# Another written-out order for attention's steps, with the combine step cut in two

## The chip, the cores and the metric

The kernel runs on one core of a Trainium2 chip. The metric is the device time of one execution in microseconds (us), as a median of runs. Matmuls run on TensorE (PE in the profile, its weight loads PEld), elementwise work on VectorE (DVE), ScalarE (ACT) and GpSimd (POOL); SyncE (SP) issues nearly all DMAs. Matmul results go to PSUM, which has eight banks here, used by number.

## The reference, cut to what matters

Three stages follow each other: an attention without softmax whose weights decay with distance, a mixture of four experts weighted by given probabilities, and a bilinear layer with an output product. All in float32.

```python
# attention: 2 batches, 8 heads, 768 positions, head size 64; per block of the sequence
intra = (q_b @ k_b.T * Dmask) @ v_b            # Dmask[i, j] = lam ** (i - j) for i >= j
out_b = intra + (q_b * lam_pow) @ kv_state
kv_state = lam_block * kv_state + (k_b * rev_pow).T @ v_b
# experts: x (1536 x 512), e = 0..3
p = probs / (probs.sum(-1) + 1e-9)
out += p[:, e] * (relu(x @ w1[e]) @ w2[e])
# bilinear
y = ((x @ wa) * (x @ wb)) @ w3 @ w_out
```

## The kernel before, in words

The kernel takes the sequence in chunks of 128 positions (six to a head) and handles two heads at a time, which makes eight units: 0 to 3 for batch 0, 4 to 7 for batch 1. `SETS` (line 57) cuts a unit's six chunks into two or three sets, so a step such as `S.5.1` is unit 5, set 1. For a set of units there are these steps, each a small function:

| word | function, line | engine | what |
|---|---|---|---|
| `qk`, `kv` | load_qk 421, load_kv 427 | SP | loads into four buffers each; the next load waits for the oldest one freed |
| `S` | scores 436 | PE | keys by queries into two banks, one a head; shape 64*128 |
| `M` | masked 452 | DVE | scores times the decay mask |
| `K` | decay 462 | ACT | keys scaled in place by a row of the mask |
| `Q` | queries 468 | POOL | queries scaled in place by `lq` |
| `U` | states 477 | PE | scaled keys by values; shape 128*64 |
| `V`, `N` | spread 489, chain 500 | ACT, DVE | the states' recurrence, one chunk a step |
| `X` | combine 511 | PE | two groups into one bank: queries by states (shape 64*64, line 520), then masked scores by values (shape 128*64, line 526) |
| `A`, `B` | attended 532 | ACT, DVE | the result out of PSUM as a rounded part and a rest |

The first four units' results for 512 tokens are the input of the experts for that third of the tokens, and the first experts are woven into the same order: `L` loads a slice of expert weights (512 KB; three raw buffers), `H` (ACT) and `D` (DVE) split it, `I.k.p` and `Y.k.p` are the in- and out-products of slice k in two halves of six full matmuls (128*128, line 122), `Z` (DVE), `HH` (ACT), `HL` (DVE) lie between them. `PB` loads the routing weights as a row for all partitions; `Z` reads it.

The preparation: `lam` loads the eight decay factors through ACT's queue and makes two constants, `zero` on DVE and `first` on POOL (line 366). `mask.h` and `lq.p` are scans on DVE, and each mask reads `first`. `half` copies the factors per pair of heads. `probs` loads the router's probabilities through ACT's queue. `route.0` sums them on POOL (four operations, lines 401 to 404), `route.1` takes the reciprocal on DVE, `route.2` multiplies on POOL, `route.3` stores the result for `PB`. `idle.12.3` runs 12 warm-up matmuls on zeros.

What sets the order is a string, `ORDER` (line 33), which the loop at line 578 walks word by word. Every engine's queue, SP's and POOL's too, takes its instructions in the order in which the words issue them; there is no reordering by a scheduler. Float32 matmuls show as two records each in the trace, so a score step of four chunks and two heads has 16. A step's last digits are its PSUM banks. After the string the kernel goes on with experts' slices 8 to 31 and the later stages, from functions that the change does not touch.

Of the kernel before, what the change touches and what calls it, by code (L numbers as in the profile page):

```python
# [43 lines left out]
A.1.1 U.3.2.5 I.2.0 K.2.1 B.1.1 qk.4.0 V.3.2 V.4.0 N.3.2.0 L.5 N.4.0.1 L.6 U.2.1.6 S.3.2.5.7 V.2.1
N.2.1.0 X.2.1.6 M.3.2 Q.3.2 X.3.2.5 kv.6.0 A.2.1 K.5.0 B.2.1 S.5.0.7.6 kv.5.1 A.3.2 I.2.1 M.5.0 Q.5.0
PB.1 L.7 B.3.2 H.5 qk.4.1 S.4.0.7.6 Z.2 qk.6.0 U.5.0.5 Q.4.0 D.5 HH.2 Y.1.0 H.6 M.4.0 I.3.0 K.6.0 D.6
V.5.0 K.5.1 X.4.0.7 HL.2 X.5.0.6 kv.4.1 A.4.0 N.5.0.1 B.4.0 H.7 U.6.0.5 kv.6.1 U.5.1.7 Y.1.1 qk.6.1
A.5.0 D.7 L.8 qk.7.0 V.6.0 V.5.1 I.3.1 B.5.0 N.6.0.1 N.5.1.0 N.5.1.1 S.6.0.6.5 Z.3 Y.2.0 K.4.1 Q.6.0
M.6.0 HH.3 N.5.1.2 K.6.1 X.6.0.6 HL.3 S.4.1.5.7 kv.7.0 A.6.0 B.6.0 U.4.1.6 M.4.1 Q.4.1 Y.2.1 L.9 V.4.1
N.4.1.0 N.4.1.1 S.7.0.5.7 N.4.1.2 X.4.1.6 M.7.0 Q.7.0 K.7.0 U.7.0.5 kv.7.1 A.4.1 U.6.1.7 I.4.0 H.8  # L50
qk.7.1 V.7.0 B.4.1 V.6.1 qk.5.1 N.7.0.1 N.6.1.0 N.6.1.1 X.7.0.6 N.6.1.2 S.6.1.5.7 A.7.0 B.7.0 I.4.1
M.6.1 Q.6.1 K.7.1 X.6.1.6 Z.4 D.8 HH.4 HL.4 S.7.1.5.7 A.6.1 B.6.1 Y.3.0 L.10 Q.7.1 M.7.1 I.5.0 Y.3.1
I.5.1 S.5.1.6.5 Z.5 U.7.1.7 M.5.1 Q.5.1 I.6.0 HH.5 V.7.1 HL.5 H.9 Y.4.0 N.7.1.0 N.7.1.1 N.7.1.2 I.6.1
# [1387 lines left out]
```

## Time and profile before

| | |
|---|---|
| median of 3 runs | 795.87 us (795.38 to 796.43) |
| the profiled execution: time, span | 796.46 us, 794.7 us |
| PE busy | 786.7 us, 99% |
| DVE, ACT, POOL busy | 547.2, 333.5, 142.7 us |
| TensorE's granted clock | full in all 40 slices |
| DMA | 95.1 MB, 120 GB/s over the span |

All rows below come from the one profiled execution. In lists by time the columns are the start, the length, the engine (SPq and ACTq are the queues that issue DMAs), the line of the kernel, the operation, its output and inputs with their shapes, and how many were merged; in square brackets stands how long the engine was idle before and what ended that. In the chain, a line is a stretch on the path that ended last, and "issue" is time in which the engine waited for nothing that the profile shows. In windows, each engine's busy time is followed by its count, in the order PE, PEld, DVE, ACT, POOL; then come the granted clock as a share of full speed, the DMA share and GB/s.

### The profile page before, as it was taken

The page shows a single profiled execution, that of the slowest core. Times are in us where ns is not written, and L with a number is a line of the kernel's source. Part 1 is how long each engine was busy: PE and PEld are TensorE (multiplying, and loading weights), DVE is VectorE, ACT ScalarE, POOL GpSimd, SP SyncE. Part 2 cuts the span into 40 slices and gives each one's busy share as a digit, 9 for nine tenths or more (in the row PEclk, how much of TensorE's full clock was granted, in tenths as well). Part 3 has the DMA queues.
Part 4 walks back from the last instruction along what each step waited for, and adds up shares of the span by engine and source line. Part 5 has one row for each costly group of instructions (what it writes and reads, how often), then busy time and mean ns, then how long its engine had stood idle before and what let it go on. Part 6 is the DMA issues. An engine that isn't in the chain of part 4 may idle for free.

```text
span 794.7 us, 10384 instructions
## 1 busy us (share of the span) xinstructions
PE 786.7 (99%) x3968; PEld 644.1 (81%) x3968; DVE 547.2 (69%) x835; ACT 333.5 (42%) x570; POOL 142.7 (18%) x107
## 2 busy tenths in 40 slices
...
GB/s 268 250 312 155 106 172 173 211 175 209 212 198 98 115 200 186 81 92 80 95 90 107 92 106 94 106 93 93 93 107 146 86 21 54 2 0 1 6 47 54
DMA packets 42178, 95.10 MB, mean 120 GB/s; under 512 B 4752, under 2 KB 10128, under 8 KB 42128
## 3 DMA queue, kind: packets, MB, share of 16 engines
...
q8 instruction: 31, 0.51, 0.2%
...
q10 hardware_dynamic: 672, 0.03, 0.1%
...
## 4 chain that ended last, share of the span: by engine, by line
PE 96%; DMA 2%; ACT 1%; DVE 0%; issue 0%; SPq 0%; ACTq 0%
PE y L122 33%; PE h L777 19%; PE h L122 11%; PE o L122 8%; PE ab L122 5%; PE a L1237 5%; PE b L1237 5%; PE w L122 5%; PE a L526 2%; PE a L443 2%; DMA w_dram<-w_sum 1%; PE a L520 1%; DMA kv<-in_kv_dram 1%; PE a L483 1%; DVE ab L1085 0%
## 5 line engine op out<-in xcount | busy, mean ns | idle before, releaser
L122 PE MATMUL y<-zp,w 128*128 128x512 f32 x768 | 186.5, 389 | 0.0
L122 PEld LDWEIGHTS y<-zp,w 128*128 128x128 f32 x768 | 144.0, 188 | 30.6 <-ACT ya L856 0.2
L227 POOL TENSOR_TENSOR cv<-cv,raw 128x512 uint32<-128x512 uint32 x40 | 65.5, 1636 | 433.5 <-DVE cv L220 391.7
L797 ACT CAST zp<-z 128x512 fp32r<-128x512 f32 x64 | 39.8, 622 | 114.8 <-DVE z L792 114.7
L122 PE MATMUL o<-w_hi,z 128*128 128x512 f32 (+1 forms) x208 | 60.1, 373 | 0.2 <-DVE z L105 0.2
L801 DVE TENSOR_TENSOR zp<-z,zp 128x512 fp32r<-128x512 f32 x64 | 44.1, 689 | 17.9 <-ACT zp L797 16.5
L319 DVE SCALAR_TENSOR_TENSOR z<-h,pb 128x512 f32<-128x512 f32 x32 | 22.1, 691 | 47.2 <-PE h L122 46.9
L122 PE MATMUL h<-xl,wh 128*128 128x512 f32 x128 | 51.0, 398 | 0.0
L122 PE MATMUL y<-hl,wh 128*128 128x512 f32 x128 | 50.5, 395 | 0.0
L122 PE MATMUL h<-xh,wl 128*128 128x512 f32 x128 | 49.9, 390 | 0.0
L122 PE MATMUL y<-hh,wl 128*128 128x512 f32 x128 | 49.9, 390 | 0.0
L122 PE MATMUL y<-hh,wh 128*128 128x512 f32 x128 | 49.9, 390 | 0.0
L326 ACT CAST hh<-z 128x512 fp32r<-128x512 f32 x32 | 19.9, 621 | 63.8 <-DVE z L319 63.8
L102 ACT CAST wh<-raw 128x1024 fp32r<-128x1024 f32 (+1 forms) x33 | 33.9, 1027 | 25.8 <-PE y L122 22.3
L122 PEld LDWEIGHTS o<-w_hi,z 128*128 128x128 f32 x208 | 37.9, 188 | 7.4 <-DVE z L105 0.5
L105 DVE TENSOR_TENSOR wl<-raw,wh 128x1024 fp32r<-128x1024 f32 (+1 forms) x33 | 39.8, 1207 | 3.4 <-ACT wh L102 3.4
L790 DVE TENSOR_TENSOR z<-h,v 128x512 f32<-128x512 f32 x16 | 11.1, 691 | 42.4 <-ACT wf L102 28.3
L105 DVE TENSOR_TENSOR w<-w,w 128x512 fp32r<-128x512 f32 x32 | 35.6, 1112 | 4.9 <-ACT w L102 4.9
L122 PE MATMUL o<-w_lo,z 128*128 128x512 f32 (+1 forms) x104 | 38.2, 373 | 0.0
L122 PE MATMUL h<-xh,wh 128*128 128x512 f32 x128 | 34.8, 390 | 0.0
L792 DVE SCALAR_TENSOR_TENSOR z<-z,pb 128x512 f32<-128x512 f32 x48 | 33.2, 692 | 1.6
L201 ACT ACTIVATE cv<-raw 128x512 f32<-128x512 f32 x40 | 26.8, 670 | 9.2 <-DMA raw<-in_w3t_dram 5.7
(227 smaller groups left out, 1655.4 us busy)
## 6 DMA issues: line engine op xcount, KB each, us to landing
...
```

The source lines that it names most:

```text
L102: act.copy(out=hi, in_=src)
L105: eng.tensor_tensor(out=lo, in0=src, in1=hi.bitcast(F32), op=ALU.subtract)
L122: lambda i=i, a=a, b=b: pe.matmul(ps, a, b, start=(first and i == 0), stop=(last and i == n - 1))
L201: act.activation(out=singles[i], in_=raws["f", i][:, :, 1].bitcast(F32), func=ACTF.Abs)
L227: pool.tensor_tensor(out=b, in0=b, in1=raws.pop(("f", i))[:, :, 0], op=ALU.add)
L319: dve.scalar_tensor_tensor(out=z, in0=h_ps.pop(k)[0], scalar=0.0, in1=pb_t[k // KF, 0], op0=ALU.max, op1=ALU.mult)
L326: act.copy(out=hh, in_=h_t[k][0])
L777: pe.matmul(chain_ps[to], w, x, start=begins and j == 0, stop=j == len(seq) - 1, skip_group_check=True,)
L792: dve.scalar_tensor_tensor(out=z, in0=src, scalar=0.0, in1=pb_t[2 * n // KF, PAIR[m]], op0=ALU.max, op1=ALU.mult)
L797: act.copy(out=t[:, 0], in_=z)
L801: dve.tensor_tensor(out=t[:, 1], in0=z_of.pop((m, f)), in1=t[:, 0].bitcast(F32), op=ALU.subtract)
L1237: pe.matmul(t, w, x, start=i == 0 and n in (1, 2, 5), stop=i == len(seq) - 1, skip_group_check=True,)
```

## The change

`combine` is cut in two: `XI` (function `inter`) holds the queries-by-states matmuls and takes the bank, `XP` the masked-scores-by-values matmuls that add to the same bank. So other steps can stand between the two halves. `ORDER` is written anew: the same steps, with every `X` as an `XI` and an `XP`, in another order and with other bank numbers. Steps whose matmuls have one shape stand next to each other more often (`U` beside `XP`, `S` beside `S`, `I` and `Y` together), unit 0's scores come first on PE, and `probs` and `route.0` stand ahead of `lam`. The diff, with the middle of both orders cut:

```diff
@@ -31,27 +31,29 @@
 ORDER = """
-kv.0.0 lam idle.12.3 qk.0.0 kv.1.0 qk.1.0 qk.2.0 qk.3.0 probs half mask.0 kv.2.0 mask.1 L.0.0 mask.2
-lq.0 kv.3.0 K.0.0 mask.3 mask.4 lq.1 U.0.0.5 mask.5 S.0.0.6.7 V.0.0 mask.6 lq.2 mask.7 route.0 lq.3
-K.1.0 M.0.0 U.1.0.4 Q.0.0 N.0.0.1 S.1.0.0.1 V.1.0 route.1 N.0.0.2 route.2 N.1.0.1 X.0.0.6 Q.1.0 M.1.0
-N.1.0.2 S.2.0.7.2 N.0.0.3 kv.3.1 A.0.0 N.1.0.3 qk.3.1 B.0.0 K.2.0 S.3.0.5.4 Q.2.0 M.2.0 X.1.0.6 H.0.0
-Q.3.0 K.3.0 M.3.0 U.2.0.7 qk.0.1 A.1.0 U.3.0.0 D.0.0 L.0.1 V.2.0 V.3.0 K.3.1 B.1.0 X.3.0.5 kv.0.1
-N.2.0.1 route.3 S.3.1.6.4 A.3.0 N.3.0.1 N.2.0.2 L.1 U.3.1.1 Q.3.1 B.3.0 X.2.0.2 V.3.1 M.3.1 N.3.1.0
-N.2.0.3 X.3.1.5 A.2.0 H.0.1 B.2.0 S.0.1.6.7 PB.0 A.3.1 D.0.1 I.0.0 Q.0.1 K.0.1 L.2 B.3.1 qk.2.1 M.0.1
...
+kv.0.0 probs route.0 lam mask.1 qk.0.0 kv.1.0 mask.0 idle.12.3 half qk.1.0 qk.3.0 K.0.0 lq.2 qk.2.0
+S.0.0.6.0 mask.3 mask.2 K.1.0 lq.0 lq.1 Q.0.0 M.0.0 mask.4 U.0.0.5 U.1.0.7 V.1.0 mask.7 N.1.0.1
+S.1.0.1.6 route.1 N.1.0.2 V.0.0 N.0.0.1 kv.2.0 N.1.0.3 Q.1.0 N.0.0.2 M.1.0 XI.0.0.3 XP.0.0 kv.3.0 mask.6
+lq.3 L.0.0 mask.5 K.2.0 qk.3.1 L.0.1 S.3.0.2.1 S.2.0.4.7 XI.1.0.6 kv.3.1 K.3.0 N.0.0.3 route.2 M.2.0
+Q.2.0 A.0.0 M.3.0 U.3.0.4 XP.1.0 U.2.0.1 V.3.0 S.3.1.5.7 N.3.0.1 K.3.1 Q.3.0 XI.3.0.0 V.2.0 U.3.1.4
+V.3.1 L.1 M.3.1 A.1.0 Q.3.1 N.2.0.1 kv.0.1 H.0.1 XP.3.0 N.2.0.2 XI.2.0.2 B.1.0 A.3.0 N.3.1.0 N.3.1.1
+N.2.0.3 qk.2.1 XI.3.1.7 K.0.1 U.0.1.5 route.3 B.0.0 V.0.1 qk.0.1 XP.3.1 A.3.1 XP.2.0 H.0.0 B.3.0 B.3.1
+kv.2.1 A.2.0 kv.1.1 kv.3.2 S.0.1.6.7 D.0.0 M.0.1 H.1 Q.0.1 B.2.0 D.0.1 L.2 N.0.1.0 K.3.2 I.0.0 PB.0
+qk.1.1 I.0.1 Z.0 K.1.1 XI.0.1.3 HH.0 D.1 H.2 HL.0 S.2.1.1.0 M.2.1 S.1.1.7.6 K.2.1 U.1.1.5 XP.0.1 qk.5.0
+qk.3.2 I.1.0 A.0.1 I.1.1 kv.4.0 L.3 V.1.1 H.3 N.1.1.0 Q.1.1 M.1.1 L.4 B.0.1 XI.1.1.3 XP.1.1 kv.5.0 D.2
+U.3.2.7 U.2.1.6 PB.1 A.1.1 Z.1 S.3.2.2.5 L.5 Y.0.0 Q.2.1 HH.1 K.5.0 V.2.1 I.2.0 V.3.2 qk.4.0 K.4.0
+N.3.2.0 N.2.1.0 Q.3.2 M.3.2 HL.1 I.2.1 XI.3.2.2 H.5 B.1.1 H.4 D.3 D.5 XI.2.1.6 qk.6.1 U.4.0.3 XP.2.1
+V.4.0 XP.3.2 A.2.1 B.2.1 U.5.0.5 L.6 N.4.0.1 Z.2 kv.5.1 A.3.2 V.5.0 S.4.0.7.6 S.5.0.4.3 B.3.2 K.5.1
+Q.5.0 M.5.0 Y.0.1 kv.6.0 Y.1.0 M.4.0 Q.4.0 L.7 D.4 N.5.0.1 qk.7.0 XI.4.0.4 K.6.0 XI.5.0.6 U.5.1.7 XP.5.0
+U.6.0.5 qk.6.0 XP.4.0 H.6 D.6 A.4.0 V.6.0 V.5.1 kv.4.1 Y.1.1 A.5.0 B.4.0 HH.2 kv.6.1 qk.4.1 B.5.0 K.6.1
+I.3.0 L.8 N.5.1.0 H.8 HL.2 N.6.0.1 N.5.1.1 I.3.1 Y.2.0 N.5.1.2 Z.3 L.9 S.6.0.6.4 Q.6.0 K.4.1 M.6.0
+S.4.1.5.7 XI.6.0.6 qk.7.1 Q.4.1 XP.6.0 U.4.1.4 A.6.0 kv.7.0 V.4.1 M.4.1 N.4.1.0 N.4.1.1 N.4.1.2 HH.3
+S.7.0.7.5 B.6.0 M.7.0 XI.4.1.6 XP.4.1 K.7.0 U.6.1.4 Q.7.0 HL.3 A.4.1 U.7.0.7 V.7.0 V.6.1 N.6.1.0 N.7.0.1
...
+D.7 Y.3.1 HL.4 Z.5 D.8 HH.5 HL.5 D.9 I.6.0 I.6.1 Y.4.0 V.7.1 L.10 Z.6 HH.6 N.7.1.0 Q.5.1 Q.7.1 I.7.0
+Y.4.1 Y.5.0 I.7.1 Y.5.1 N.7.1.1 N.7.1.2 M.5.1 XI.7.1.6 XI.5.1.7 Z.7 HH.7 XP.7.1 A.7.1 B.7.1 HL.6 XP.5.1
+A.5.1 HL.7 B.5.1
 """
...
@@ -508,9 +510,8 @@
             op1=ALU.add,
         )
 
-    def combine(u, s, to):
+    def inter(u, s, to):
         c0, _, n, _ = chunks(u, s)
-        kvt, pt = kv_t.pop((u, s)), p_t.pop((u, s))
         qd = qk_t.pop((u, s))[:, 0].rearrange("p (c i) -> p c i", c=n)
         ps = bank(to, "a")[:, : n * P].rearrange("p (c i) -> p c i", c=n)
         c1 = 0 if c0 else 1
@@ -521,13 +522,18 @@
                     ps[r, c, :], entering(u, s, c)[r], qd[r, c, :],
                     start=c == c1, stop=False, skip_group_check=True,
                 )
+        x_ps[u, s] = ps
+
+    def combine(u, s):
+        _, _, n, _ = chunks(u, s)
+        kvt, pt = kv_t.pop((u, s)), p_t.pop((u, s))
+        ps = x_ps[u, s]
         for c in range(n):
             for j in range(2):
                 pe.matmul(
                     ps[j * D : (j + 1) * D, c, :], kvt[:, 1, c, j, :], pt[:, j, c, :],
                     start=False, stop=True, skip_group_check=True,
                 )
-        x_ps[u, s] = ps
 
     def attended(u, s, low):
         b, hp = divmod(u, HP)
@@ -561,7 +567,8 @@
         "U": states,
         "V": spread,
         "N": chain,
-        "X": combine,
+        "XI": inter,
+        "XP": combine,
         "A": lambda u, s: attended(u, s, False),
         "B": lambda u, s: attended(u, s, True),
         "L": lambda j, *half: load_half(*half) if half else load("j", j),
```

## Rows read from the trace of the kernel before

**Rows 1.** The page: TensorE's busy time, and the chain that ended last.
```profile
PE 786.7 (99%) x3968; PEld 644.1 (81%) x3968; DVE 547.2 (69%) x835; ACT 333.5 (42%) x570; POOL 142.7 (18%) x107
...
PE 96%; DMA 2%; ACT 1%; DVE 0%; issue 0%; SPq 0%; ACTq 0%
```

**Rows 2.** Windows by stage: stretch, its length, busy time of each engine.
```profile
0.00:94.00 94.00, 91.91 (x897) 72.32 (x898) 52.99 (x114) 35.65 (x80) 16.13 (x27) 1.00 0.68 227
94.00:200.00 106.00, 104.86 (x462) 86.48 (x462) 83.96 (x127) 59.63 (x92) 24.72 (x19) 1.00 0.51 182
200.00:400.00 200.00, 198.58 (x870) 162.80 (x871) 149.34 (x224) 91.51 (x149) 22.10 (x13) 1.00 0.43 138
400.00:600.00 200.00, 200.00 (x879) 163.84 (x878) 151.32 (x234) 79.97 (x135) 18.64 (x9) 1.00 0.28 93
```

**Rows 3.** The chain in order of time: start us, us, what.
```profile
12.90 1.54 PE a L443 x24
14.44 0.83 PE a L520 x12
15.27 1.02 PE a L526 x16
...
16.99 0.36 issue
...
18.38 0.65 PE a L443 x8
...
23.05 1.59 PE h L122 x6
...
35.93 0.59 PE a L526 x8
36.52 0.35 PE a L483 x12
...
57.71 0.50 PE a L483 x12
...
75.78 1.36 PE h L122 x6
```

**Rows 4.** Instructions of POOL in order of time, the start.
```profile
1.06 0.29 POOL L366 TENSOR_SCALAR_AFFINE_SELECT first<-zero 128x128 f32<-128x128 f32 x1 [0.63 <-DVE zero L364]
5.69 0.40 POOL L401 TENSOR_TENSOR dsum<-dp 128x12 f32<-128x12 f32 x1 [4.34 <-DMA dp<-in_probs_dram]
...
6.80 0.26 POOL L404 TENSOR_SCALAR dsum<-dsum 128x12 f32<-128x12 f32 x1
```

**Rows 5.** Instructions of DVE in order of time, the start.
```profile
3.71 0.34 DVE L388 COPY lamq<-lamb 64x4 f32<-64x4 f32 x2 [2.73 <-DMA lamb<-in_lam_dram]
4.08 1.05 DVE L381 TENSOR_TENSOR_SCAN mask<-lamb,first 128x128 f32<-128x128 f32 x3
...
8.30 1.29 DVE L459 TENSOR_TENSOR p<-a,mask 128x512 f32<-128x512 f32 x2 [0.32 <-PE a L443]
9.51 0.27 DVE L502 SCALAR_TENSOR_TENSOR st<-st,lq,a 128x64 f32<-128x64 f32 x1
```

**Rows 6.** Instructions and DMA issues of ACT in order of time, the start.
```profile
0.71 0.40 ACTq L363 DMA_DIRECT2D lamb<-in_lam_dram  x1
...
1.21 0.39 ACTq L397 DMA_DIRECT2D dp<-in_probs_dram  x1
...
8.34 0.91 ACT L466 ACTIVATE kv<-kv,mask 128x256 f32<-128x256 f32 x2 [0.91 <-DMA kv<-in_kv_dram]
```

**Rows 7.** Instructions of PE in order of time, the start.
```profile
8.90 1.08 PE L483 MATMUL a<-kv 128*64 128x64 f32 x16 [0.63 <-ACT kv L466]
9.91 1.16 PE L443 MATMUL a<-qk 64*128 64x128 f32 x16
11.00 0.87 PE L520 MATMUL a<-qk,st 64*64 64x128 f32 x12
```

**Rows 8.** The DMA issues of SP in order of time, 48 to 66 us.
```profile
56.70 0.54 SPq L430 DMA_DIRECT2D kv<-in_kv_dram  x1
...
62.58 0.55 SPq L430 DMA_DIRECT2D kv<-in_kv_dram  x1
```

**Rows 9.** The tile kv: from issue to landing over all its loads.
```profile
DMA to landing us min/median/max: 3.0/5.8/7.9
```

**Rows 10.** Instructions of ACT in order of time, 50 to 70 us.
```profile
60.76 0.69 ACT L466 ACTIVATE kv<-kv,mask 128x128 f32<-128x128 f32 x2 [3.71 <-DMA kv<-in_kv_dram]
...
66.69 0.80 ACT L466 ACTIVATE kv<-kv,mask 128x192 f32<-128x192 f32 x2 [0.65 <-DMA kv<-in_kv_dram]
```

**Rows 11.** Windows with the DMA rate, in GB/s, last.
```profile
8.50:12.50 4.00, 3.53 (x56) 3.03 (x58) 3.27 (x10) 0.96 (x3) 2.18 (x3) 1.00 1.06 404
30.00:33.50 3.50, 3.50 (x22) 2.59 (x24) 2.74 (x5) 2.25 (x7) 0.87 (x1) 1.00 1.06 387
38.00:44.00 6.00, 6.00 (x62) 4.10 (x63) 1.82 (x6) 1.33 (x4) 1.19 (x2) 1.00 0.93 271
44.00:50.00 6.00, 6.00 (x64) 4.52 (x66) 4.49 (x7) 4.38 (x9) 0.46 (x1) 1.00 1.01 347
...
61.50:62.50 1.00, 1.00 (x24) 1.00 (x25) 0.00 (x0) 0.00 (x0) 0.00 (x0) 1.00 0.00 0
```

More of the change, by code (lines that the diff above doesn't have):

```diff
@@ L39 @@
-N.2.0.1 route.3 S.3.1.6.4 A.3.0 N.3.0.1 N.2.0.2 L.1 U.3.1.1 Q.3.1 B.3.0 X.2.0.2 V.3.1 M.3.1 N.3.1.0
-N.2.0.3 X.3.1.5 A.2.0 H.0.1 B.2.0 S.0.1.6.7 PB.0 A.3.1 D.0.1 I.0.0 Q.0.1 K.0.1 L.2 B.3.1 qk.2.1 M.0.1
-H.1 L.3 U.0.1.5 I.0.1 N.3.1.1 kv.4.0 V.0.1 N.0.1.0 D.1 kv.1.1 qk.1.1 X.0.1.6 Z.0 L.4 qk.3.2 HH.0 I.1.0
-kv.3.2 A.0.1 HL.0 H.2 kv.2.1 B.0.1 S.2.1.7.5 D.2 I.1.1 Q.2.1 qk.5.0 H.3 M.2.1 Y.0.0 K.4.0 D.3 K.1.1
-S.1.1.6.7 Z.1 U.1.1.5 Q.1.1 Y.0.1 V.1.1 M.1.1 HH.1 H.4 N.1.1.0 HL.1 X.1.1.6 K.3.2 D.4 U.4.0.7 kv.5.0
@@ L44 @@
[L44 to L53, printed above, removed]
@@ L54 @@
-D.9 Y.4.1 Z.6 HH.6 I.7.0 HL.6 Y.5.0 I.7.1 Y.5.1 Z.7 HH.7 X.5.1.6 HL.7 X.7.1.5 A.5.1 B.5.1 A.7.1 B.7.1
+kv.0.0 probs route.0 lam mask.1 qk.0.0 kv.1.0 mask.0 idle.12.3 half qk.1.0 qk.3.0 K.0.0 lq.2 qk.2.0
+S.0.0.6.0 mask.3 mask.2 K.1.0 lq.0 lq.1 Q.0.0 M.0.0 mask.4 U.0.0.5 U.1.0.7 V.1.0 mask.7 N.1.0.1
+S.1.0.1.6 route.1 N.1.0.2 V.0.0 N.0.0.1 kv.2.0 N.1.0.3 Q.1.0 N.0.0.2 M.1.0 XI.0.0.3 XP.0.0 kv.3.0 mask.6
+lq.3 L.0.0 mask.5 K.2.0 qk.3.1 L.0.1 S.3.0.2.1 S.2.0.4.7 XI.1.0.6 kv.3.1 K.3.0 N.0.0.3 route.2 M.2.0
@@ new lines @@
+U.6.0.5 qk.6.0 XP.4.0 H.6 D.6 A.4.0 V.6.0 V.5.1 kv.4.1 Y.1.1 A.5.0 B.4.0 HH.2 kv.6.1 qk.4.1 B.5.0 K.6.1
+I.3.0 L.8 N.5.1.0 H.8 HL.2 N.6.0.1 N.5.1.1 I.3.1 Y.2.0 N.5.1.2 Z.3 L.9 S.6.0.6.4 Q.6.0 K.4.1 M.6.0
+S.4.1.5.7 XI.6.0.6 qk.7.1 Q.4.1 XP.6.0 U.4.1.4 A.6.0 kv.7.0 V.4.1 M.4.1 N.4.1.0 N.4.1.1 N.4.1.2 HH.3
+S.7.0.7.5 B.6.0 M.7.0 XI.4.1.6 XP.4.1 K.7.0 U.6.1.4 Q.7.0 HL.3 A.4.1 U.7.0.7 V.7.0 V.6.1 N.6.1.0 N.7.0.1
+Y.2.1 N.6.1.1 N.6.1.2 S.6.1.5.7 M.6.1 H.9 Q.6.1 Y.3.0 H.7 I.4.0 B.4.1 XI.6.1.6 XI.7.0.7 qk.5.1 XP.7.0
```

1 line of the change is left out of this document (added).

## Prediction

> **What bounds the kernel now.** I read the page first. TensorE is busy for 99% of the span, and the chain that ended last is 96% PE [rows 1]; beside TensorE no engine passes 69%. So the time is PE's work plus the few moments in which PE waits. The windows by stage come next [rows 2]: the attention order that is changed fills the first 94 us (the first group of the next stage starts at 93.9), and PE is idle there for about 2.1 us: 1.04 before its first matmul, 0.63 for a decay on ACT, 0.36 at 17.0 us. From 94 to 600 it idles 2.6 us in 506. That later part keeps its instructions and their order and runs at PE's pace, so a microsecond won or lost before 94 us arrives at the end whole. I take nothing from behind it.
>
> Then I read the chain in order of time, where one line is a run of matmuls of one shape and its length is start to next start [rows 3]. There the price of a shape shows. Scores (64*128): 24 records take 1.54, 8 take 0.65, so 55.6 ns each and 0.205 per run. The inter products (64*64): 0.83 for 12, of which I take 0.055 each and 0.145 per run (the 0.02 to 0.03 left is the edge of the merging). The intra products and states share 128*64: 1.02 for 16 and 0.59 for 8 give 54 ns and 0.15 per run; a states group of 12 costs 0.50 after another shape but 0.35 right after intra products, which is the 0.15 saved. Expert groups (128*128) of 6 take 1.59 between other shapes and 1.36 among their own kind, 0.225 per run.
>
> **The gain.** I split both orders into runs of one shape. Before there are 75: 17 inter, 26 states-or-intra, 16 scores, 16 full (warm-up counted). After there are 49: 12, 14, 13, 10. The instructions are the same ones (XI and XP are the two halves of X). So the price falls by 5 x 0.145 + 12 x 0.15 + 3 x 0.205 + 6 x 0.225 = 0.73 + 1.80 + 0.62 + 1.35 = 4.5 us. This is PE time on the path, nothing covers it, and I take it as certain to about 0.5.
>
> **What is late next: the start.** In the new order `route.0` stands ahead of `lam`, so on POOL the four small operations on the router's sums stand ahead of `first`, and every mask scan on DVE reads `first`. Before, `first` ran at 1.06; the sums could start at 5.69 only, since their 24 KB landed then, 4.4 us after the issue at 1.21, and took 1.37 to 7.06 [rows 4, 6]. After, the load is issued at 0.71 and lands near 5.1, the sums end at 6.5, `first` at 6.8, and the masks begin 2.8 us later than the 4.08 of before [rows 5]. From here with durations of before: mask.1 and mask.0 end at 7.6 (0.33 apart, 0.40 the last); K.0.0 takes 0.91 on ACT [rows 6], to 8.5; `half`, lq.2, mask.3 and mask.2 end at 8.9, K.1.0 then at 9.85; U.1.0 follows (16 records, 0.46) to 10.3, S.1.0 (1.09) to 11.4. PE has nothing else queued ahead of these: S.0.0 fills only 1.1 us. The inter products of unit 0 then need the third state, N.0.0.2. On DVE ahead of it: lq.0 and lq.1 (0.64), M.0.0 (1.21 apart from the next), mask.4 and mask.7 (0.65), the reciprocal and five chain steps of 0.2, the last 0.27 long; it ends at 12.55. XI.0.0 ends at 12.8 and XP.0.0 (1.02) at 13.85. Before, PE had the same five steps behind it at 12.9 less 0.07 [rows 3, 7], that is 12.83. One run is saved in this stretch (0.15, counted above), so the waits here are 1.15 us more than before's. If the 24 KB land at 4.6 it is 0.65; if `first` were not held at all, 0. The lam values, issued second now, land by about 5 (2.9 after their issue before [rows 4 to 6]) and are hidden behind `first`. The swap of qk.3.0 and qk.2.0 and the later L.0.0 cost nothing here: their users run after 13.8, the loads are issued by 6.
>
> **What is late next: loads.** SP issues loads in order, and each waits for its buffer. The trace shows how long one takes when little is ahead of it [rows 8 to 10]; its rows carry lines, so I name loads by counting them in the order: kv.7.1 (512 KB) is issued at 62.58 and ACT, waiting for it, starts at 66.69, so 4.1; kv.7.0 (256 KB) 56.70 to 60.76, so 4.06. At 370 GB/s (387 and 404 in two full stretches, 271 to 347 in others [rows 11]) the bytes are 1.4 and 0.7, and a fixed 2.7 to 3.35 is left. The shortest landing of all kv loads is 3.0, so a fixed 2.3 is the low end. I take 2.7, from kv.7.1, since nothing moved in the microsecond before it [rows 11], and 0.2 from the freeing matmul to the issue. Now PE's work between the event that frees the buffer and the use, with the prices above, against the load's path:
> (a) qk.1.1 for S.1.1: behind the end of XP.2.0 go kv.3.2, L.2, PB.0 and itself, 1.31 MB. Path 0.2 + 2.7 + 3.5 = 6.4. PE has S.0.1 0.65, I.0.0 and I.0.1 2.95, XI.0.1 0.59, S.2.1 0.65 and 0.24 of small waits = 5.1. Wait 1.4.
> (b) kv.5.1 for U.5.1: from XI.3.2's end, qk.6.1, L.6 and itself, 1.57 MB: 0.2 + 2.7 + 4.25 + decay 0.85 = 8.0. PE: XI.2.1 0.44, U.4.0 to U.5.0 1.48, two scores 1.09, two Y groups 2.95, two inter 0.59 = 6.55. Wait 1.4.
> (c) U.4.1: its decay K.4.1 now stands on ACT behind H.8, which waits for L.8. From XP.5.0's end kv.4.1, kv.6.1, qk.4.1, L.8, 2.1 MB: 0.2 + 2.7 + 5.7 + H.8 0.95 + decay 0.85 = 10.4, less 0.67 of PE work before XP.4.0 ends = 9.7; PE from there to U.4.1 has 5.67 + 1.54 + 0.37 + 0.59 = 8.2. Wait 1.5.
> (d) U.7.0 behind qk.7.1 and kv.7.0: 5.8 against 4.0 plus the 1.5 of (c): wait 0.35.
> (e) U.0.1: kv.0.1 is freed by XP.1.0; 0.2 + 2.7 + 0.7 + decay 0.64 = 4.25 against 3.5 of PE work. Wait 0.7.
> Sum 5.35. I.1.0 also hangs on PB.0: D.1 stands on DVE behind Z.0, which needs the router row. That path (7.5 from XP.2.0) just fits behind (a)'s wait, so it costs nothing more, but up to 0.8 if (a) vanishes. Small waits for banks (a product group that needs a bank DVE or ACT has not emptied yet) I put at 0.45. Before's 0.36 at 17.0 us goes. Bounds of the load waits: 0 and 8.
>
> **Sum.** -4.5 + 1.15 + 5.35 + 0.45 - 0.36 = +2.1 us on the profiled 796.46 (span 794.7 and 1.76 around it), 798.6. That run lies 0.6 above the median 795.87 of the three, so the forecast in the median's terms is 798.0.
>
> **A rule weighed.** The trace's loads leave 2.7 us beside their bytes at 370 GB/s [rows 8 to 11]. The Trainium skill, page DMA: Bandwidth & Descriptors, section Anatomy of one DMA, fits a load (on GpSimd's path) as about 2.0 us fixed plus its bytes at 436 GB/s. By that the five waits would be 1.05 together, by estimate, and the sum -2.2. The rows here come from SP's queue with its own backlog, and they decide for me.
>
> **Rivals.** (1) Loads in time: if buffers come free about 1.4 us earlier relative to the use, or the fixed part is nearer 1.5, none of (a) to (e) waits: -4.5 + 1.15 + 0.45 - 0.36 = -3.3, 792.6. For it: the fastest landing is 3.0 [rows 9]. Against: every load on which ACT is seen waiting took over 4. (2) A draw: fixed 2.3 and 404 GB/s shorten the five waits to 0.67 + 0.69 + 0.66 + 0.56 + 0.26 = 2.84, sum -0.4, 795.5. It decides below a fixed 2.4. (3) Heavier: fixed 3.35, as kv.7.0 shows, adds 0.65 to (a), (b), (e) and to (c) with (d): +2.6, so +4.7, 800.6; for it also the 271 GB/s of 38 to 44 us. (4) The change doesn't do what it says, because the 0.15 to 0.225 belong to each step's own start and not to the change of shape: then nothing is saved, +6.6, 802.5. The states group that costs 0.35 after intra products and 0.50 elsewhere speaks against it.
>
> **How the numbers follow.** Forecast 0.44 (its own range 796.8 to 799.3, half a microsecond on each of a few waits), rival 1 0.20, rival 2 0.20, rival 3 0.13, rival 4 0.03. What a measurement of this kernel can tell from no change is about 0.2%, 1.6 us. Slower by more than that, above 797.5: two thirds or more of the forecast's cases, with rivals 3 and 4 and a few of rival 2, 0.53. Faster, below 794.3: most of rival 1 and a part of 2, 0.22. Within: 0.25. The range leaves out the far ends of rivals 1 and 3: 793.0 to 800.4.
>
> **What would show it.** Right: the first scan at 6.5 to 7 us; XP.0.0 ending near 13.8; PE waiting at S.1.1, U.5.1, U.4.1 and U.7.0 for loads or for the decays behind them, 3.5 us or more in all; the next stage starting near 96; runs of 24 scores at 1.54 and so on. Wrong: PE's idle time before the next stage below 4 us, or that stage starting before 93; or a run of states after intra products at no less than 0.50 for 12.

## The result, and the profile after

The changed kernel takes 806.98 us as a median of four runs (802.08 to 809.04), beside 795.95 before: a ratio of 1.013, 95% interval 1.0084 to 1.0176. I had forecast 798.0 in 793.0 to 800.4. The profiled execution took 807.36 (span 805.6), 10.9 more than the one of before. One run of the version h1_warm_both below took 1317.6 us at a mean granted clock of 0.557 and is left out of every comparison.

The page first [rows 1]: TensorE's busy time, its granted clock in 40 slices, and the chain's shares by engine.

```profile
PE 789.4 (98%) x3968; PEld 647.9 (80%) x3968; DVE 545.6 (68%) x835; ACT 333.1 (41%) x570; POOL 143.0 (18%) x107
...
PEclk9899999999999999999999999999999999999999
...
PE 87%; DMA 7%; DVE 3%; ACT 1%; issue 1%; SPq 1%; ACTq 0%; DVEq 0%
```

PE does the same work and is busy 2.7 us longer; DMA's share of the chain is 7% in place of 2%; and a digit of the clock that was 9 before is 8. The windows by stage [rows 2] say where:

```profile
0.00:94.00 94.00, 84.96 (x810) 68.44 (x811) 50.68 (x111) 34.06 (x77) 16.34 (x27) 0.95 0.65 214
94.00:200.00 106.00, 106.00 (x516) 87.81 (x515) 76.42 (x117) 57.99 (x89) 23.14 (x17) 1.00 0.49 172
200.00:400.00 200.00, 196.86 (x864) 161.24 (x863) 148.82 (x222) 90.71 (x148) 21.50 (x14) 1.00 0.45 145
```

In the first 94 us PE is idle for 9.0 us in place of 2.1. The chain in order of time [rows 3] shows that the next stage starts at 103.14 and not at 93.92, so 9.2 of the 10.9 us arise ahead of it:

```profile
1.43 6.67 DMA qk<-in_qk_dram
...
8.15 1.92 PE a L445 x16
10.07 1.90 PE a L485 x32
...
24.58 0.54 SPq L432
...
25.16 0.60 SPq L165
...
25.86 0.38 SPq L305
...
26.28 5.98 DMA qk<-in_qk_dram
...
32.39 1.23 PE a L445 x8
...
34.88 4.92 PE h L124 x12
...
55.85 0.44 PE a L533 x8
56.28 0.23 PE a L485 x8
...
82.57 0.50 PE a L485 x12
...
99.34 1.90 PE a L521 x32
101.24 1.90 PE a L533 x32
103.14 2.04 PE h L124 x8
```

Read the lengths. Sixteen score records took 1.09 before; here they take 1.92 at 8 us. Twelve expert records (one group pair) take 2.95 between other shapes; at 34.88 they take 4.92. Late in the order (82.57 on) every run has the price that I had put on it. Windows with TensorE alone (stretch, length, busy time, granted clock, DMA share, GB/s) name the reason:

```profile
8.00:12.00 4.00, 3.85 (x50) 0.57 1.06 402
...
9.00:11.00 2.00, 2.00 (x29) 0.50 1.06 398
...
12.00:32.00 20.00, 17.31 (x232) 1.00 0.84 262
32.00:40.00 8.00, 7.61 (x37) 0.57 0.50 180
40.00:103.00 63.00, 60.40 (x560) 1.00 0.57 189
```

A clock of 0.57 is one of 1.00 (2.4 GHz) for a part of the window and 0.50 (1.2 GHz) for the rest; a window inside the first stretch, 9 to 11 us, has 0.50 throughout. I call such a stretch a fall of the clock. 4 us less 0.57 of them is 1.7 us lost, and 8 us less 0.57 is 3.4. Ahead of both stretches TensorE had stood idle for more than 2 us. These are its waits in order of time (in brackets the idle time and what ended it):

```profile
8.15 1.92 PE L445 MATMUL a<-qk 64*128 64x128 f32 x16 [2.32 <-DMA qk<-in_qk_dram]
...
20.45 0.68 PE L485 MATMUL a<-kv 128*64 128x64 f32 x7 [0.26 <-ACT kv L468]
...
25.22 0.72 PE L445 MATMUL a<-qk 64*128 64x128 f32 x8 [0.67 <-DMA qk<-in_qk_dram]
...
32.39 1.23 PE L445 MATMUL a<-qk 64*128 64x128 f32 x8 [2.13 <-DMA qk<-in_qk_dram]
...
50.15 1.44 PE L445 MATMUL a<-qk 64*128 64x128 f32 x14 [1.08 <-ACT xf L545]
...
63.97 1.16 PE L445 MATMUL a<-qk 64*128 64x128 f32 x16 [0.70 <-DMA qk<-in_qk_dram]
66.64 0.91 PE L485 MATMUL a<-kv 128*64 128x64 f32 x12 [0.56 <-ACT kv L468]
...
70.82 0.74 PE L485 MATMUL a<-kv 128*64 128x64 f32 x8 [0.24 <-ACT kv L468]
```

**An account of it.** For every run of one shape I take the time from its first record to the first record of the next run and subtract its price from the prediction (start price plus records; a state record 0.029). What is left is a stall, whether the trace shows it as idle time or inside a run. Before, 71 of 75 runs lie within 0.12 us of their price and the stalls sum to 1.9; after, 35 of 49 do, and the stalls sum to 13.8. The first attention step starts at 8.15 in place of 6.35. So 9.2 = -4.5 (prices) + 1.8 (start) + 11.9 (stalls), and of these stalls 5.1 are time lost by steps at 1.2 GHz. The other 1.7 us come behind the next stage. The experiments below make versions of both kernels; the table has the account of the main ones ("next stage" and "stalls" from one trace, "behind" its span less the next stage, "low" the us lost to 1.2 GHz ahead of the next stage, "time" the median):

| version | runs of one shape | stalls | low | next stage | behind | time |
|---|---|---|---|---|---|---|
| before | 75 | 1.9 | 0 | 93.9 | 700.9 | 796.0 |
| before, pairs grouped | 69 | 2.4 | 0 | 93.2 | 700.0 | 796.1 |
| before, more grouped | 66 | 5.4 | 0 | 96.0 | 700.5 | 797.9 |
| changed | 49 | 13.8 | 5.1 | 103.1 | 702.5 | 807.0 |
| changed, factors first | 49 | 14.1 | 1.7 | 102.3 | 701.3 | 804.3 |
| changed, five kv buffers | 49 | 9.3 | 1.7 | 98.6 | 701.9 | 803.0 |
| changed, repaired | 49 | 8.2 | 0 | 97.1 | 701.0 | 800.2 |

### The profile page after: what moved, and what is told of

The parts are those of the page before. It is cut to its first block, busy times and chain, and to the rows that moved or that the text cites. A ratio compares the mean times of both kernels' runs of the same rounds, so it can differ in the third digit from the quotient of the medians.

```text
span 805.6 us, 10349 instructions
## 1 busy us (share of the span) xinstructions
PE 789.4 (98%) x3968; PEld 647.9 (80%) x3968; DVE 545.6 (68%) x835; ACT 333.1 (41%) x570; POOL 143.0 (18%) x107
## 4 chain that ended last, share of the span: by engine, by line
PE 87%; DMA 7%; DVE 3%; ACT 1%; issue 1%; SPq 1%; ACTq 0%; DVEq 0%
PE y L124 30%; PE h L784 18%; PE h L124 9%; PE o L124 8%; PE a L1244 5%; PE b L1244 5%; PE ab L124 4%; PE w L124 4%; DMA qk<-in_qk_dram 2%; PE a L445 1%; DMA kv<-in_kv_dram 1%; PE a L533 1%; DMA w_dram<-w_sum 1%; PE a L521 1%; PE a L485 1%
```

## The experiments

Times are medians; the kernel before, run beside each, had medians of 796.1 to 796.5. In parentheses stands the ratio to it with its 95% interval.

**The two gaps and the start.** Four versions of the changed kernel, one edit each. The ratio intervals of all four overlap that of the changed kernel (1.0084 to 1.0176), so by the time alone none of them can be told from it; what they show is in their traces.

```diff
# e1_warm_start
-idle.12.3
+idle.18.3
# e2_warm_mid
-S.2.1.1.0 M.2.1 S.1.1.7.6
+S.2.1.1.0 M.2.1 idle.5.7 S.1.1.7.6
# e3_qk11_early
-kv.1.1 kv.3.2 S.0.1.6.7
+kv.1.1 qk.1.1 kv.3.2 S.0.1.6.7
...
-PB.0 qk.1.1 I.0.1
+PB.0 I.0.1
# e4_lam_first
-kv.0.0 probs route.0 lam mask.1
+kv.0.0 lam probs route.0 mask.1
```

> The changed kernel with 18 warm-up products in place of 12 (each two records of 0.2 us), so that TensorE is busy until about 8.2 us, when the load of the first queries and keys lands; no wait is removed. In the changed kernel TensorE stood idle from 5.82 to 8.15 and then ran at 1.2 GHz until 11.8: 16 score records and 32 state records took 3.72 us, about 1.6 more than at full clock. Theory A (the fall of the clock is paid in full): granted clock 1.00 in the first 22 us, these records take 2.1, everything behind comes 1.6 earlier, 805.4 against 807.0 for the changed kernel, and the next stage starts near 101.5. Theory B (the low clock costs nothing because the recurrence on VectorE or the loads behind it are late anyway): clock full, the same 48 records shorter, but the wait turns up as a new idle time before 25 us; next stage at 103, 807. Theory C (the clock falls for what the engine does after the gap and not for the gap): low stretch still there, 807.

> The changed kernel with five warm-up products (about 2.0 us) put between the scores of unit 2 set 1 and those of unit 1 set 1, where TensorE waited 2.13 us for a load (30.26 to 32.39); the load lands no earlier. In the changed kernel the clock is at 1.2 GHz from 32.3 to 39.2: 34 records that would take 4.4 us at full clock took 7.4. Theory A: clock full there, 3.0 us gained, 804.0, next stage near 100. Theory B (later waits take it back: 1.08 at 50.2, 0.70 at 64.0, 0.56 at 66.6 grow): clock full, but the gain is under 1.5, 805.5 to 807. Theory C: clock falls all the same, 807.

> The changed kernel with the load of unit 1 set 1's queries and keys put ahead of unit 3 set 2's keys and values (which waits for a buffer until 24.6), of an expert slice and of the routing weights' row. It is issued near 23.5 in place of 27 and lands by about 28.5, ahead of its scores at 30.3. Theory A (wait and clock both cost): the wait of 2.13 and the low clock behind it go, 5.1 us gained less what the three loads behind it lose (0.6 us later, one of them possibly a wait of up to 0.7): 802 to 802.6, next stage near 98.5. Theory B (only the wait counts): 804.9. Theory D (the loads share one rate, so that a wait of 2 us or so appears at another load): 806 to 807, and the trace shows that wait at the products of the first expert slice or at unit 3's states.

> The changed kernel with the decay factors' load and the mask constants ahead of the router's load and sums again, as in the kernel before; the rest of the new order stays, scores first. In the changed kernel the factors landed at 6.8 (5.5 after their issue; 2.9 before) and the first mask scan began at 6.82 (4.08 before); but TensorE waited from 5.82 to 8.15 for the load of the first queries and keys. Theory A (that load sets the start): first scan near 4, first decay near 6.5, yet the first scores again near 8.1 after a gap of 2.3 us, clock low behind it, 806.5 to 807. Theory E (the order of the two small loads also holds up the large ones: the DMA rate dipped to 130 GB/s between 3.9 and 6.3): the queries and keys land by about 7.1 as before, the gap is 1.3, the clock stays full, and 2.5 us are gained: 804.5. My prediction of record put the whole start at 1.15 us by the masks: by that the time would be 805.9.

e1 took 803.98 (1.0102, 1.0066 to 1.0137). The gap at the start is 1.31 and the clock stays up; the 48 records take 2.90 in place of 3.72 and not 2.1, since the second state step now shows a wait of 0.73 for its decay, which the slow clock had hidden. The next stage starts at 100.4, earlier than theory A has it. Here are its windows, with a wait of 1.67 later on that was followed by a fall (31 to 35 us):

```profile
5.00:8.00 3.00, 1.85 (x17) 1.00 0.79 280
8.00:15.00 7.00, 6.67 (x108) 1.00 1.01 368
29.00:31.00 2.00, 0.79 (x12) 1.00 0.91 298
31.00:35.00 4.00, 3.55 (x23) 0.57 0.19 66
```

e2 took 805.42 (1.0112, 1.0076 to 1.0147). The middle gap has 1.09 us of idle time left and a full clock behind it, but the start's fall, which the edit does not touch, was twice as long in this execution (3.4 us lost between 7.8 and 14.6), so the next stage came at 102.6, and this trace settles nothing between the theories.

e3 took 806.38 (1.0129, 1.0087 to 1.0171). The wait of 2.13 is gone, the trace has no fall, and the next stage starts at 98.9, as theory A has it. But 0.82 and 0.63 appear at the second expert slice, whose routing row went out behind that load: a part of theory D. The median gained nothing that can be measured; the profiled execution, at 803.62, was the shortest of the four.

e4 took 804.29 (1.0089, 1.0065 to 1.0113), as theory E has it. The first instructions on DVE and PE:

```profile
3.98 0.74 DVE L383 TENSOR_TENSOR_SCAN mask<-lamb,first 128x128 f32<-128x128 f32 x2 [3.00 <-DMA lamb<-in_lam_dram]
...
7.04 1.16 PE L445 MATMUL a<-qk 64*128 64x128 f32 x16 [1.43 <-DMA qk<-in_qk_dram]
```

The large load lands 1.1 us earlier although its place in SP's queue is the same. In the windows from 4 to 6 us the DMA engines move 117 GB/s in the changed kernel and 362 here (367 before):

```profile
4.00:6.00 2.00, 1.62 (x12) 1.43 (x11) 1.95 (x8) 0.35 (x1) 0.14 (x1) 1.00 1.10 362
```

All eight traces with the router's load first have 79 to 123 GB/s there, all others over 300. So the swap of two small loads made a hole of about 2 us in the large ones. Unit 0's last combine step ends at 12.93 (12.83 before), against 14.02 in e1: the swap costs 1.1 us at full clock. How two small loads do this is not shown. The later wait for unit 1 set 1 grew to 2.89 here, with a fall behind it, and took a part back.

**Buffers, and all repairs together; the clock in the kernel before; fewer groupings.**

```diff
# f1_five_kv (changed kernel)
+    kv_p = opened(att, "kvp", 5)
-        t = unit_p.tile([P, 2, 4, 2, D], F32, tag="kv", name="kv")[:, :, :n]
+        t = kv_p.tile([P, 2, 4, 2, D], F32, tag="kv", name="kv")[:, :, :n]
# f2_repaired: f1, e3, e4, and
-idle.12.3
+idle.15.3
...
-H.5 B.1.1 H.4 D.3 D.5
+B.1.1 H.4 D.3
...
-A.3.2 V.5.0
+A.3.2 H.5 D.5 V.5.0
# f4_before_gap (kernel before)
-idle.12.3
+idle.6.3
# g1_before_pairs (kernel before, X cut in two)
-XI.2.0.2 XP.2.0 V.3.1 M.3.1 N.3.1.0 N.2.0.3 XI.3.1.5 XP.3.1
+XI.2.0.2 V.3.1 N.3.1.0 M.3.1 N.2.0.3 XI.3.1.5 XP.2.0 XP.3.1
...
```

> The changed kernel, order untouched, with five buffers for keys and values in place of four (the other four tiles of queries and keys stay). In the changed kernel the loads on SyncE stood behind keys and values that waited for a buffer which the later intra products free (13.6 us of such waits, 8 times); so the load of unit 1 set 1 went out only at 27 and its scores waited 2.13. Theory A (the grouped order holds each buffer longer, and that makes the load waits): the stalls at the scores near 25, 32 and 64 us and at the states near 66 and 71 fall from 4.3 us in all to under 1.5, the gap of 2.1 and the low clock behind it are gone, next stage near 97.5 to 99, time 801 to 802. Theory D (the rate is the limit: the first 32 us move 260 GB/s on average with stretches at 400): stalls move to other loads and stay above 3 us, 805 to 807.

> The changed kernel with all that was found put right at once: decay factors' load ahead of the router's; 15 warm-up products, to 7.0 us; five buffers for keys and values; the load of unit 1 set 1's queries and keys ahead of unit 3 set 2's keys and values; on ScalarE the fourth expert slice split ahead of the fifth, and the fifth behind unit 3's last result (the bank that a score step at 50 us waited for 1.1 us). The runs of one shape stay as in the change. Theory A (the saving of 4.5 us by fewer changes of shape is real, and waits and the clock hid it): full clock, stalls before the next stage under 3 us, that stage starting at 93 or before, 793 to 796. Theory F (the saving is not there: every step pays its start wherever it stands): with stalls of 3 us the next stage starts no earlier than 95.5, 798 or more. Theory D (the loads' rate): stalls of 5 us or more are left, 799 to 802.

> The kernel before with 6 warm-up products in place of 12 and nothing else changed: TensorE stands idle from about 3.5 to 6.35, when its first states begin as before. This measures the clock by itself, with the old order and the old loads. Theory A (a gap of 2 to 3 us is followed by 1.2 GHz, and that is paid): granted clock 0.5 for 4 to 7 us from 6.4 on, the steps of this stretch at double length, the next stage 1.5 to 3 us later than 93.9, 798 to 799.5. Theory B (work at the start waits for masks, decays and loads anyway): low clock, but under 0.8 us later, 796.4 to 797.2. Theory C (the gap does not lower the clock): full clock, 796.4.

> The kernel before's order with the combine step cut in two, and at three places (units 2 and 3 near 20 us, units 4 and 5 near 50, units 5 and 7 at the end) the two inter products put together and then the two intra products: six runs of one shape fewer, no load moved past another. By the prices per run 3 x 0.145 + 3 x 0.15 = 0.9 us are saved if no wait comes in: next stage near 93.0, 795.5 against 796.4. Theory F (the price belongs to the step, not to the change of shape): 796.4. Theory D (even here buffers come free later and loads fall behind): stalls of 0.5 us or more near 25 to 35 us, 796.5 to 798.

f1 took 802.96 (1.0086, 1.0071 to 1.0101), below a second measurement of the changed kernel (1.011 to 1.0157, further down); its next stage starts at 98.6. The stalls fall to 9.3. The load of unit 1 set 1 goes out at 24.4 in place of 26.3, but with the loads ahead of it takes 6.4 us, and its scores, which come earlier too, still wait 1.92, with a fall behind. So the buffers are a part of the cause: the next stage comes when theory A has it, while the time, 1 us above its range, and the wait that is left at that load speak for a part of theory D.

f2 took 800.19 (1.0046, 1.0035 to 1.0058), the clock full in all its runs. Waits of PE between 25 and 66 us:

```profile
30.36 0.50 PE L124 MATMUL h<-xl,wh 128*128 128x512 f32 x1 [0.55 <-DVE z L321]
...
31.75 0.50 PE L124 MATMUL h<-xh,wl 128*128 128x512 f32 x1 [0.89 <-DVE wl L107]
...
46.55 0.50 PE L124 MATMUL y<-hl,wh 128*128 128x512 f32 x1 [1.11 <-DVE p L462]
...
60.83 0.91 PE L486 MATMUL a<-kv 128*64 128x64 f32 x12 [0.70 <-ACT kv L469]
```

None of these waits ends directly with a load, yet the stalls of the whole order are 8.2 us, more than the 4.5 saved. Two of them are loads at second hand, 2.4 together: the first expert's weighting on DVE waits for the routing row until 29.6, and the decay at 60.8 stands on ACT behind an expert slice. The others are steps of DVE, ACT and POOL that have less work of another shape to hide behind. The score steps of units 4 and 5 in a row need four banks, one of them an output bank; the output products stand until DVE has emptied it (1.4). The next stage at 97.1 is as late as theory F wants, but its reason falls: the runs without a stall have their prices. Time and stalls lie in the ranges of theory D, but of the 8.2 us only those 2.4 are traced to loads.

f4 took 798.56 (1.0025, 1.0015 to 1.0036). Its trace has a gap of 2.16 us, and these windows behind it:

```profile
7.00:15.00 8.00, 7.70 (x80) 0.57 0.84 318
15.00:40.00 25.00, 24.64 (x269) 1.00 0.72 233
```

The old order with the old loads loses 3.4 us at 1.2 GHz, and its next stage starts at 96.2, 2.3 later: theory A by the trace. A second trace of the same kernel (800.61) has it again, from 7.4 to 14.3, and the next stage at 96.6:

> The kernel before with 6 warm-up products once more, for a second trace. Eight of its ten runs have a mean granted clock above 0.997 and still stand about 2 us above the kernel before. If the clock's fall after the gap is the whole cost, a run with a full clock starts its next stage at 93.9 +- 0.3; if the start itself is later for another reason (masks, decays, loads), the trace shows the stall before 18 us at full clock.

But eight of its first ten runs have a mean granted clock above 0.997, and seven of these still lie 1.1 us or more above the kernel before, so the fall is not the whole price of this gap; no trace here is of such a run, and what they pay stays open.

g1 took 796.14 (0.9998, 0.9989 to 1.0006). Every grouped run has its price, 0.9 us less; new stalls of 0.4 at 24 us and 0.15 at the start take the rest, and the next stage starts at 93.2 in place of 93.9. In the time it cannot be told from no change.

**One grouping undone, and more groupings.**

```diff
# f5_ungroup (f2)
-S.4.0.7.6 S.5.0.4.3 B.3.2 K.5.1 Q.5.0 M.5.0 Y.0.1 kv.6.0 Y.1.0 M.4.0 Q.4.0 L.7
+S.4.0.7.6 B.3.2 K.5.1 Q.4.0 M.4.0 Y.0.1 kv.6.0 S.5.0.7.6 Q.5.0 M.5.0 Y.1.0 L.7
...
-N.5.1.0 H.8 HL.2
+N.5.1.0 HL.2
...
-K.4.1 M.6.0
+K.4.1 H.8 M.6.0
# g2_before_more (g1)
-K.1.0 M.0.0 U.1.0.4 Q.0.0 N.0.0.1 S.1.0.0.1 V.1.0
+K.1.0 N.0.0.1 N.0.0.2 M.0.0 U.1.0.4 Q.0.0 V.1.0
...
-XP.0.0 Q.1.0 M.1.0 N.1.0.2
+XP.0.0 S.1.0.0.1 Q.1.0 N.1.0.2 M.1.0
...
-S.2.1.7.5 D.2 I.1.1 Q.2.1 qk.5.0 H.3 M.2.1 Y.0.0 K.4.0
+D.2 I.1.1 qk.5.0 H.3 Y.0.0 S.2.1.2.3 Q.2.1 M.2.1 K.4.0
```

> The repaired version (factors' load first, longer warm-up, five buffers for keys and values, earlier loads), in which two more places are changed. One grouping is undone: the scores of unit 5 no longer stand right behind those of unit 4, where both needed four banks, one of them a bank of the first experts' output, and the output products behind them waited for the mask of unit 5 (1.4 us); they go between two groups of output products and use unit 4's banks again. That adds two changes of shape, 0.205 + 0.225. And the decay of unit 4 set 1 goes ahead of the split of expert slice 8 on ScalarE, behind whose load it stood (1.27 us at the states of that set). Theory G (with loads and clock repaired, what is left of the stalls is the grouping itself: dependent steps stand closer, with less work between them): 1.4 - 0.43 + about 1.1 less, next stage near 95.0 in place of 97.1, 798.1. Theory D (the loads' rate is the limit): the stalls move to other loads, next stage at 96.5 or later, 799.5 to 800.2.

> The version of the kernel before with its three pairs grouped, and two more places. At the start unit 1's scores go behind unit 0's combine steps and join the scores of units 2 and 3 (0.205), so that unit 0's inter products follow unit 1's states at 9.4 and not at 10.9; the two recurrence steps they need go ahead of unit 0's mask on VectorE. Near 30 us the scores of units 2 and 1 stand together behind the first output products (0.205 + 0.225), into two banks that the output needs only later. Prices: 0.64 of shape changes less, and up to 0.6 of the waits before 10 us; by these the next stage starts at 92.0 to 92.6 against 93.9 before and 93.2 with the pairs alone, 794.6 to 795.2 against 796.4. Theory D (the first 20 us are set by the loads): the gain at the start returns as stalls at the states of units 2 and 3, next stage at 92.8 or later, 795.4 or more.

f5 took 800.73 (1.0059, 1.0041 to 1.0076), the same as f2 within the intervals. Its trace is of its slowest run (803.53). Both stalls fell (1.4 to 0.9, 1.27 to 0.15), but a wait of 2.35 for the decay of unit 7, with a fall of the clock behind it, and two waits on loads (1.56 and 1.42) came in. Theory G is not borne out: in this trace what the two places gave came back at loads and at a decay that stood behind a load, as theory D has it.

g2 took 797.91 (1.0023, 1.0014 to 1.0032): slower. It has 66 runs, and the stalls rose by 3.5 us to 5.4 against 1.5 saved (0.9 by the pairs, 0.64 by the two places). Three of its waits:

```profile
14.45 0.96 PE L445 MATMUL a<-qk 64*128 64x128 f32 x8 [0.67 <-DVE kept L504]
...
36.98 0.44 PE L521 MATMUL a<-qk,kept 64*64 64x128 f32 x4 [0.77 <-DVE p L461]
...
55.81 0.72 PE L445 MATMUL a<-qk 64*128 64x128 f32 x8 [0.62 <-DMA qk<-in_qk_dram]
```

Two of the three are for DVE's work on the steps that were pushed together.

**The price of the clock in the total.**

```diff
# h1_warm_both (changed kernel); h1_again is the same, after_again the changed kernel
-idle.12.3
+idle.19.3
...
-S.2.1.1.0 M.2.1 S.1.1.7.6
+S.2.1.1.0 M.2.1 idle.6.7 S.1.1.7.6
# c1_gap (kernel before); c2_gap_warm has nine products on zeros ahead of the last one
+        pe.matmul(ps, zero, zero, start=True, stop=True)
+        dve.tensor_copy(out=first, in_=ps)
+        for _ in range(5):
+            pool.tensor_tensor(out=first, in0=first, in1=zero, op=ALU.add)
+        pe.matmul(ps, first, zero, start=True, stop=True)
```

> The changed kernel with warm-up products in both gaps (19 in place of 12 at the start, 6 more in front of unit 1 set 1's scores); order, loads, buffers and waits otherwise as in the change. It separates the clock from the waits: in the changed kernel's trace the steps at 1.2 GHz took 4.7 us longer than at full clock. Theory A (the clock is a cost of its own, some 4.7 of the 10.9 us): full clock in the first 45 us, stalls of about 9 us left, next stage at 98.0 to 98.8 against 103.1, 802.0 to 802.8, with less spread from run to run than the 802.1 to 809.0 of the changed kernel. Theory B (later waits take it back): full clock, next stage after 100.5, 804.5 to 807.

> The changed kernel once more, on the same chip and beside the version with warm-up products. Its first four runs lay at 802.1 to 809.0, median 807.0. Expected 805 to 808, runs with a full mean clock at 802 to 803. If the trace falls full again, its next stage starts at 103 +- 1; stalls of 13 to 14 us with 4 to 5 of them in steps at 1.2 GHz.

> The changed kernel with warm-up products in both gaps, beside the changed kernel in the same call. Theory A (the clock is paid in full): 4 to 5 us below it. Theory A' (half of it is taken back by waits on loads and for small results that the slow steps had hidden, as its first trace showed: stalls 10.6 with those inside the warm-up against 13.8): 2.5 to 3.5 below. Theory B: within 1 us of it.

> The kernel before with a gap put in at one place, at the very end of the attention order (92 to 97 us): a small product, its copy on VectorE, five small additions in a row on GpSimd, and a small product that reads their result, so that TensorE stands idle for some 2.5 us; all else as before. Theory A (a gap of that length is followed by a stretch at 1.2 GHz whose lost time arrives at the end): granted clock 0.5 for 3.5 to 7 us behind the gap, and 1.7 to 3.5 us above the version of the same gap filled with small products, that is 800.5 to 802.5. Theory B (the lost time is made up by work that waits anyway): clock low, but under 0.8 us above the filled one, 799 to 799.5. Theory C (the gap does not lower the clock): full clock, 799.

> The same gap in the kernel before, with nine small products (18 records) in it, so that TensorE is busy for most of it; the product behind it starts no earlier. All theories: full clock, 796.4 plus the gap of about 2.5 us, 798.8 to 799.4. It is the measure for the open gap.

h1 took 806.17 (1.0116, 1.009 to 1.0141) and 806.91 (1.0133, 1.0115 to 1.0151) the second time; the changed kernel beside it 805.66 (1.0133, 1.011 to 1.0157). Its next stage starts at 100.3 and 99.7, with no fall ahead of it, against 103.1 and 104.5. So the gaps' falls cost the early part some 3 to 5 us, and the medians kept none of it. In its second trace the clock fell at 231 us, behind another wait; in the first, 703.9 us lie behind the next stage, 1.4 more than in the changed kernel. By the time theory A is not borne out. Up to the next stage the traces lie between A (98.0 to 98.8) and B (after 100.5): a part of the gain was taken back there. The traced executions were shorter (805.9 and 804.6 against 807.4 and 810.0), the medians were not.

c1 took 801.30 (1.0066, 1.0053 to 1.0078), c2 802.62 (1.0082, 1.0068 to 1.0095). The gap is 3.5 us from product to product in both. The windows around it, c1 first:

```profile
93.00:97.00 4.00, 1.49 (x20) 1.00 0.39 131
97.00:102.00 5.00, 4.47 (x14) 0.66 0.00 0
```

```profile
93.00:97.00 4.00, 3.48 (x36) 1.00 0.38 131
97.00:102.00 5.00, 4.75 (x22) 1.00 0.00 0
```

By itself c1 adds up as theory A has it: 796.1 + 3.5 (the gap) + 1.7 (the fall) = 801.3. But theory A also put c1 1.7 to 3.5 above c2, and c2 came out 1.3 longer (the intervals overlap), so by the time theory A is not borne out here either. In the traces c2 is 1.9 us ahead behind the gap (0.3 of it from before the gap), and 1.8 behind at the end: its clock fell later, at 230 us, behind a wait of 2.0 for a sum of the weights' product, these waits were 3.4 us in place of 2.2, and 0.9 more is lost near 320 us. So filling the gap saved at the gap and, in the one trace, gave it back later; why the median of c2 is no shorter is open. The last two kernels, the one before with 13 and with 11 warm-up products (`idle.13.3`, `idle.11.3`), ask whether the mere number of small products does it:

> The kernel before with 13 warm-up products in place of 12: two records more, 0.2 to 0.4 us, which end at 6.6 or so against the 6.35 at which the first states began. By the chain the time is 796.3 to 796.7. If the number of products in front shifts the waits on the stores and loads of 190 to 240 us by itself, 798 or more.

> The kernel before with 11 warm-up products in place of 12: TensorE stands idle for about 0.3 us ahead of its first states, no more; nothing else starts later. By the chain 796.2 to 796.5 and a full clock. If fewer products in front shift the rest by themselves, 797.5 or more, as in the eight runs of the version with 6 that show no fall of the clock.

It does not: 796.46 (0.9996, 0.9988 to 1.0005) and 796.47 (1.0006, 0.9996 to 1.0015).

## Why the prediction was wrong, by its steps

**The gain** was right: 4.5 us. Of 49 runs, 35 stand within 0.12 of their price; 32 inter records take 1.90 (0.145 + 32 x 0.055 = 1.905). Eight state records right behind intra products take 0.23 (56.28 above): 8 x 0.029, with no start of their own. Rival 4 falls.

**The start** was right in size (1.15; e1 less e4 gives 1.1, and the step that I put at 13.85 ends at 14.02 in e1 and 13.78 in e3, which kept the clock up there; in the changed kernel's own trace, with the fall, at 14.85), but not in cause: that the first scan came at 6.82, as I had said, was luck. I expected the router's sums to hold `first` until 6.8; they were done at 3.9, and the factors themselves landed at 6.8 only, in the hole that their own swap made. I had called the factors' landing hidden, and the first queries' load was not in my list at all.

**The loads** were the right mechanism, mis-sized and partly misplaced. (a) was put at 1.4 and took 2.1, in the second trace of the same kernel 3.2; (c) 1.5 and 1.1; (d) 0.35 and 0.7; (e) 0.7 and under 0.3; (b) never came. For (a) the chain shows the term: the buffer is free at 24.58, and the load goes out at 26.28, behind three other issues on SP; I had 0.2 for these 1.7 us. From there to landing it took 6.0, and I had 6.2. Not on my list: scores at 25.2 and 64.0 us (0.9 and 1.0 with the restart), and 1.8 at 50 us, where a score step waits for a bank that ACT empties behind an expert slice whose load lands at 47.7. A run that a wait breaks also pays a part of its start again: 0.97 us of stall at 64 us for 0.70 of idle time. All waits together, with the start, were 8.6 us by the account (13.7 less 5.1 at the low clock), where I had 6.6.

**The clock** is the step that failed by most: the sum took every duration from a trace at full clock [rows 2] and let a wait cost no more than itself. In each of the changed kernel's two traces 5.1 us are lost at 1.2 GHz (all ahead of the next stage in the first, 3.4 of it there and 1.7 at 213 us in the second), about 0.7 of it over a wait that was there anyway. Its nine runs sort by it: at a mean clock of 0.994 they took 806.6 to 810.0 (five runs), at 0.996 to 0.998 804.5 to 805.7 (three), at 1.000 802.1. The same holds where nothing was edited: of the 88 runs of the kernel before that ran beside the versions, the 84 at 0.999 or 1.000 have a median of 796.3, and the four at 0.995 to 0.998 took 798.2 to 800.7, longer by about the time lost at the lower clock. That goes with the clock and does not prove it the cause, since longer waits bring the falls. The Trainium skill (TensorE: Matmul & The Clock Gate, What's actually happening) has the array run at half its clock until it has been busy for a while, and fall back when it idles. The traces agree on the two levels, 1.00 and 0.50 in the windows above, and on falls behind idle time, though not every wait brought one; I had not weighed it. The clock is not all, either: the one run of the changed kernel at a full clock still took 802.1, 4.1 above the forecast and outside its range. No trace is of that run; that of e3, also at a full clock and 803.62 long, has its next stage at 98.9 and 702.9 us behind it, so there waits and the later part alone make the miss. And since h1 and c2 kept the clock up at the gaps and were no shorter, how much of the median the clock costs stays open.

**Behind 94 us** I took nothing. The changed kernel's traces have 702.5 and 703.7 us behind the next stage, the kernel before 700.9. That stretch is not all PE's: the chain from 200 to 235 us runs through stores and loads, and PE waits there twice for a sum (the changed kernel's first of these waits, then that of the kernel before).

```profile
202.66 6.84 DMA w_dram<-w_sum
...
215.55 4.94 DMA t_dram<-w
...
220.50 5.14 DMA w<-in_w_dram
```

```profile
210.22 0.50 PE L124 MATMUL w<-wol,w3h 128*128 128x512 f32 x1 [2.13 <-ACT w_sum L622]
```

```profile
200.24 0.50 PE L122 MATMUL w<-wol,w3h 128*128 128x512 f32 x1 [1.38 <-ACT w_sum L615]
```

Lined up matmul by matmul, the changed kernel's trace loses 0.6 of the 1.7 at these two waits, 0.35 near 428 us and 0.7 near 663. The two waits differ from execution to execution: together 2.6 us in the trace of the kernel before, 1.6 to 3.9 over the 20 traces. So a part of the 1.7 may be no effect of the change; with one or two traces of each version that stays open. In h1's first trace they were 3.9, and near 661 us a further 1.4 was lost; so it gave back 1.4 of the 2.8 us by which its next stage was earlier than the changed kernel's.

So 10.9 = 2.1 (forecast) + 2.0 (waits) + 5.1 (clock) + 1.7 (behind), in the one trace.

**The rule weighed.** The Trainium skill (DMA: Bandwidth & Descriptors, Anatomy of one DMA) gives a load on GpSimd's path 2.0 us plus its bytes, 2.6 for 256 KB by estimate. The trace does not agree for this queue: the load at 26.28 took 5.98, with three others beside it. My price for the four together (2.7 fixed, 3.5 for their bytes) was near that; what I had not priced was the time until its issue.
